# Sliding-window attention with a gated feed-forward on one core: GpSimd's clearings among VectorE's normalizations, dummy matmuls regrouped, reload waits added

## The chip, the core and the metric

The kernel runs on one core of one Trainium2 chip. Its time is the device time of one execution in microseconds; less is better. A run's time is that of a whole execution; a profile takes one execution apart, and its span is somewhat shorter than that execution's time.

## What is computed

`x` is 2048 x 576 (bf16). The result is `x + s * g`, both from the same normalized rows:

```python
xn = _layernorm(x, axis=-1)             # no scale, no shift
s = _A_ref(xn, A_wqkv, A_wo)            # attention, 32 heads of 18, window of 256 keys, causal, then wo
g = _silu(_B_ref(xn, B_w_gate, B_w_up, B_w_down))   # (sigmoid(xn Wg) * (xn Wu)) Wd, inner size 4608
return x + s * g
```

## The kernel before, in words

The 2048 rows are worked in four chunks of 512, each chunk in four blocks of 128 rows. A chunk goes through: layer norm and a transpose of the normalized rows (`xnr` to `xn`, so that the features lie on the partitions); projections to queries, keys and values; the feed-forward's gate and up projections with the attention's scores and products laid between their matmuls; the output projection and the down projection; the final combination. Weights stream from memory through rings of buffers on SyncE's DMA queue.

**Who sets the order.** The program is a list of operations (`Op`), each with an engine, a planned duration, dependencies `deps` (a semaphore wait where engines differ) and `odeps` (order for the planner alone: the operation is planned after them, but no wait is put into the program). `schedule` plays the list through with the planned durations and priorities (`prio`, lower goes first) and so fixes the order of the instructions on each engine; `emit` writes them out in that order and adds the waits. A wait that an engine has made before is not written again. `slack` is added to the planned landing of a DMA.

**The opening** is what the change touches, that is chunk 0 up to the first feed-forward matmul:

- For each of the four blocks, VectorE makes two statistics (`bn_stats`, L509 and L511, one for each half of a row) and their combination (L513); GpSimd takes a power of the variance for 1/sqrt (L516, `rstd`); VectorE normalizes (L526, a `tensor_scalar` from bf16 to bf16 with two scalars per row). TensorE transposes (L552, ten small matmuls), ScalarE copies the result from PSUM to `xn` (L565).
- Between these, TensorE runs dummy matmuls on a buffer of ones (`warm`, L422), in groups `w0`, `w1`, `w2` of 8, 3 and 2 pairs (`WARM`), and the first projections (L608), each in three steps such as `q0.0`, `q0.1`, `q0.2` for the queries of block 0. Step `.0` needs the first half of that weight matrix, step `.1` the rest, and so a wait for DMAs. The order on TensorE is written out by hand in the string `OPEN`; `t0` to `t3` are the transposes.
- Buffers have to be cleared or filled once: `pk` on ScalarE (L413, one activation that writes zeros); three parts of `expr`, as `ez0` on VectorE and `ez1`, `ez2` on GpSimd (L386, 128 x 1024 f32 each); the ones beside the values, `vones` and `vpad` on GpSimd (L408, L409); the mask `m64`, by a memset (L397) and three `affine_select` (L400) on GpSimd and a copy on VectorE (L403). Before, GpSimd's order is: identity matrix and small constants, `ez1`, the four powers, then `ez2`, the mask's memset, `vones`, `vpad`, the three selects. The list `op_late` puts `ez2`, the mask's memset and `vones` behind the last power.
- Projected queries and keys go from PSUM to `pk` and `expr` in halves on ScalarE and VectorE (L679), values to `vau` (L726). VectorE also copies some blocks of `xn` from one half of the partitions to the other (L576), for the feed-forward.

**Reloads.** The projection weights lie in one layout for chunk 0 and are loaded again in another for the later chunks (`build_again`, eight DMAs during chunk 0's feed-forward). In the later chunks each projection depends on all eight (L594). The projections of chunk 1 stand on TensorE between the two halves of chunk 0's down projection (L1152): its row blocks 0 and 1 come before them, blocks 2 and 3 after.

Of the kernel before, what the change touches and what calls it, by code (L numbers as in the profile page):

```python
# [9 lines left out]
H = 32  # L10
DH = 18
# [93 lines left out]
OC_SLACK = 3000.0  # L105
LATE_SLACK = 5000.0
LN_STEP = 8
OPEN = """w0 t0 w1 t1 q0.0 w2 q0.1 q1.0 q1.1 t2 q0.2 q1.2 q2.0 q2.1 v0.0 v0.1 t3 q2.2 v0.2 q3.0 q3.1 v1.0 v1.1 q3.2 v1.2
v2.0 v2.1 v3.0 v3.1 v2.2 v3.2 k0.0 k0.1 k1.0 k1.1 k0.2 k1.2 k2.0 k2.1 k3.0 k3.1 k2.2 k3.2"""
OPEN_Y = ("q2", "v0", "v2", "v3", "k2", "k3")  # L110
QKV_AGAIN = 15
AGAIN_PRIO = 6
N_FACTOR = 1.2
# [5 lines left out]
TH_PRIO = 0  # L119
HM_PRIO = -1  # L120
QKT_BEHIND = {3: 0, 4: 1}
WARM = (8, 3, 2)
X0_SLACK = (-250.0, 150.0, 400.0, 900.0)
QKV_SLACK = 300.0
X_PRIO = (-20, -19, -18, -7.9)
X_EXTRA = (1.0, 1.0, 1.3, 1.3)
Q_SLACK = 0.0
QKV_LOAD = (-8, -6, -7)
W_PRIO = (-5, -4, -3, -2)
WARM_NS = 427.0  # L130
# [101 lines left out]
class Builder:  # L232
# [16 lines left out]
    def op(self, eng, occ, fn, name, deps=(), prio=3, **kw):  # L249
        o = Op(eng, occ, fn, name, deps, prio, **kw)  # L250
        o.cidx = len(self.ops)
        self.ops.append(o)
        return o
# [78 lines left out]
    def build(self):  # L332
        self.r_xr = Ring(NXR)
        self.r_xnr = Ring(NXNR)
        self.r_xn = Ring(1)
        self.r_w = Ring(RW)
        self.r_t = Ring(RT)
        self.r_pk = Ring(RPK)
        self.r_exp = Ring(NEXP)
        self.r_s = Ring(RS)  # L340
        self.r_xf = Ring(RXF)
        self.r_kd = Ring(RKD)
        self.r_rec = Ring(RREC)
        self.r_bn = Ring(RBN)
        self.op_f1 = {}
        self.op_proj, self.op_open = [], {}
        self.build_init()
        self.op_pv = [[None] * NHG for _ in range(NCH)]
        self.op_sc = [[[] for _ in range(NHG)] for _ in range(NCH)]
        self.op_on = [[None] * NHG for _ in range(NCH)]  # L350
        self.op_mul = [[None] * NHG for _ in range(NCH)]
        self.all_kd = {}
        self.op_oc = [[[], []] for _ in range(NCH)]
        self.op_v = [None] * NQB
        self.op_tail = [None] * NHG
        self.op_hT = {}
        self.f2_last = None
        self.op_out = []
        for c in range(NCH):
            self.build_ln(c)  # L360
            if c == 0:
                self.build_weights()
                self.build_wd()
            self.build_qkv(c)
            self.last_mul = None
            self.build_attn(c)
            self.load_x(c)
            self.op_pkz = [self.op("POOL", 2000, lambda e: e.memset(self.pk[:, 1:RPK, :, :], 0.0), f"pkz:{c}",
                                   deps=self.op_on[c], prio=1)]
            if c == 0:  # L370
                self.op_wo = []
            self.build_wo(c)
            self.build_ffn(c)
            if c == 0:
                self.build_again()
                self.build_late_weights()
                for o in self.ops:
                    if o.name in ("wo:0:00", "wo:0:10"):
                        o.add_dep(self.op_wo)
                for k, o in enumerate(self.op_wo):  # L380
                    self.f2_ops[(1, k % 5)].add_dep(o)

    def build_init(self):
        op = self.op
        self.op_pre = op("DVE", 450, lambda e: e.memset(self.hT[:, 0, :], 1.0), "pre", prio=-9)
        ez = [op(eng, 1000, lambda e, k=k: e.memset(self.expf[:, 2 * k:2 * k + 2, :, :], 0.0), f"ez{k}", prio=p)  # L386
              for k, (eng, p) in enumerate((("DVE", -8), ("POOL", 0), ("POOL", 0)))]
        self.op_ez = ez
        self.op_negh = op("POOL", 60, lambda e: e.memset(self.neghalf[:, :], -0.5), "neghalf", prio=-5)
        ep = op("POOL", 60, lambda e: e.memset(self.bnst[:, :, 12:14], 0.0), "eps0", prio=-5)  # L390
        self.op_eps = op("POOL", 60, lambda e: e.memset(self.bnst[:, :, 14:15], EPS * D), "eps1", deps=[ep], prio=-5)
        id1 = op("POOL", 200, lambda e: e.memset(self.op_[:, NOT - 1, 0:P], 1.0), "id1", prio=-6)
        self.op_ident = op("POOL", 300, lambda e: e.affine_select(
            self.op_[:, NOT - 1, 0:P], self.op_[:, NOT - 1, 0:P], pattern=[[1, P]], compare_op=ALU.is_equal, fill=0.0,
            base=0, channel_multiplier=-1), "id2", deps=[id1], prio=-4)
        ez[1].odeps.append(self.op_ident)
        m1 = op("POOL", 300, lambda e: e.memset(self.m64[:, :, :], 1.0), "m1", prio=0)  # L397
        self.op_late = [ez[2], m1]
        for k in range(3):
            m1 = op("POOL", 200, lambda e, k=k: e.affine_select(  # L400
                self.m64[0:64, k, :], self.m64[0:64, k, :], pattern=[[-1 if k == 1 else 1, 64]], compare_op=ALU.is_ge,
                fill=0.0, base=-(k % 2), channel_multiplier=1 if k == 1 else -1), f"m2:{k}", deps=[m1], prio=3)
        self.op_mask = [op("DVE", 130, lambda e: e.tensor_copy(self.m64[64:P, :, :], self.m64[0:64, :, :]), "m3", deps=[m1],  # L403
                           prio=2)]
        h0 = op("DVE", 70, lambda e: e.memset(self.hm[:, :], 0.0), "hm", prio=4)
        self.op_hm = [op("DVE", 70, lambda e, q=q: e.memset(self.hm[32 * q:32 * q + 32, q % 2:q % 2 + 1], 1.0),
                         f"hm:{q}", deps=[h0], prio=4) for q in range(4)]
        vo1 = op("POOL", 1100, lambda e: e.memset(self.vau[:, :, :, 0:H // 2, DH:DH + 1], 1.0), "vones", prio=1)  # L408
        self.op_vones = op("POOL", 300, lambda e: e.memset(self.vau[:, :, :, H // 2, :], 1.0), "vpad", deps=[vo1], prio=1)  # L409
        self.op_late += [vo1, h0]  # L410
        for k, n in enumerate(WARM):
            self.op_open[f"w{k}"] = self.warm(n, f"warm:{k}", [self.op_pre] if k == 0 else [], mm_ns(CH) if k else WARM_NS)
        self.op_pkz = [op("ACT", 1300 + 1000, lambda e: e.memzero(self.pk[:, 0:2, :, :]), "pkz", prio=-30)]  # L413

    def warm(self, n, name, deps, ns):
        ps = Psum((6, 7))
# [21 lines left out]
    def build_weights(self):  # L438
        wq = self.wqkv
        self.op_wqn = [[] for _ in range(3)]  # L440
        for j in range(3):
            c0 = j * D
            nat = self.wqn[:, j, 0:4 * D].rearrange("p (k c) -> p k c", k=4)
            for k in (0, 2):
                r0 = k * P + (64 if k else 0)
                self.op_wqn[j].append(self.dma(
                    nat[:, k:k + 2, :], wq[r0:r0 + 2 * P, c0:c0 + D].rearrange("(k p) c -> p k c", p=P),
                    N_FACTOR * 2 * P * D * 2, f"wqn{j}.{k}", ("wqkv", j, k // 2), prio=QKV_LOAD[j], issue=W_ISSUE_NS))
            for h in range(2):
                self.op_wqn[j].append(self.dma(  # L450
                    self.wqn[64 * h:64 * h + 64, j, 4 * D:4 * D + HV], wq[MID * 64:MID * 64 + 64, c0 + h * HV:c0 + (h + 1) * HV],
                    W_FACTOR * D // 2 * P, f"wqn{j}.{4 + h}", ("wqkv", j, 2 + h), prio=QKV_LOAD[j]))
            for o in self.op_wqn[j]:
                o.slack = QKV_SLACK
        o = self.op_wqn[0][0]
        o.eng, o.prio, o.slack = "ACT", -40, Q_SLACK
        o.add_dep(self.op_pre)
        self.op_pkz[0].behind.append(o)
# [34 lines left out]
    def build_ln(self, c):  # L493
        op = self.op
# [3 lines left out]
        for i in range(QPC):  # L498
            st = c * QPC + i
            if c == 0:  # L500
# [6 lines left out]
                           prio=X_PRIO[i] if c == 0 else 4, slack=X0_SLACK[i] if c == 0 else LATE_SLACK)  # L507
# [16 lines left out]
            if c == 0:  # L524
                out = out.rearrange("p (g c) -> p g c", g=2)
            ap = op("DVE", 400 if c == 0 else 350, lambda e, st=st, xs=xs, out=out: e.tensor_scalar(  # L526
                out, xs, self.mv[:, st, 0:1], self.rstd[:, st, :], ALU.subtract, ALU.mult), f"apply:{st}",
                deps=[rs, ag] + dr, prio=pr)
            ring.release(sx, ap)
            if c > 0:  # L530
                wr = op("DVE", 100, lambda e, sr=sr: e.tensor_copy(self.xnr[:, sr, D:DP], self.xnr[:, sr, 0:64]),
                        f"wrap:{st}", deps=[ap], prio=pr)
            if st == QPC - 1:
                self.op_mask[0].odeps.append(ap)
                for o in self.op_late:
                    o.odeps.append(rs)
            tok = slice(i * P, (i + 1) * P)
            if c > 0:
                for k, (i0, i1, col) in enumerate(((0, NKT, 0), (NKT, NC, 64))):
                    o = self.dma(self.xn[:, i0:i1, tok], self.xnr[:, sr, col:col + (i1 - i0) * P],  # L540
                                 XT_BYTES * (i1 - i0) * P * P * 2, f"xt:{st}.{k}", ("xt", i, k), deps=[wr, ap] + dxn,
                                 prio=-2, issue=XT_ISSUE_NS, transpose=True)
# [975 lines left out]
```

## Time and profile before

| | |
|---|---|
| median of 3 runs | 560.14 us (560.14 to 560.2) |
| the profiled execution's own time | 560.04 us |
| its span | 558.3 us |
| TensorE busy (matmul) | 552.4 us, 99% |
| VectorE, ScalarE, GpSimd busy | 318.9, 274.9, 32.1 us |
| DMA | 74.24 MB, mean 133 GB/s |

The span runs from the first instruction to the last. An engine's busy time counts its compute instructions, not its waits. In a timeline each line gives start and duration in us, engine, source line, operation, output and inputs, count, and in brackets how long the engine stood idle before it and what ended that. PE is TensorE, PEld its weight loads, DVE VectorE, ACT ScalarE, POOL GpSimd, SP SyncE; a q behind a name is its instruction queue.

### The profile page before, as it was taken

How to read it: one execution, taken by the hardware profiler on the slowest of the kernel's cores; microseconds unless marked ns; L12 is line 12 of the kernel's file. 1: busy time of each engine (PE TensorE's matmuls, PEld its weight loads, DVE VectorE, ACT ScalarE, POOL GpSimd, SP SyncE). 2: the span in 40 equal slices, each digit the busy share in tenths (PEclk: the TensorE clock that was granted, in tenths of full speed). 3: DMA queues.
4: the chain of work that ended last, by engine and by line, in shares of the span. 5: the costliest groups of instructions: out<-in, count | busy, mean ns of one | idle time of the engine just before them, and what ended most of it. 6: DMA issues, size and time to landing. Idle time of an engine off the chain costs nothing.

```text
span 558.3 us, 18736 instructions
## 1 busy us (share of the span) xinstructions
PE 552.4 (99%) x8128; PEld 312.9 (56%) x8130; DVE 318.9 (57%) x906; ACT 274.9 (49%) x388; POOL 32.1 (6%) x61
## 2 busy tenths in 40 slices
PE   7999999999999999999999999999999999999998
PEld 4755555569555555546755555545665555554554
DVE  7536997506066986633507699844430785786111
ACT  4426786114066785702407678740330875774031
POOL 5001110100000110010000011001000000000100
PEclk9999999999999999999999999999999999999999
DMA  8999999936956765314995656422479365651010
GB/s 232 221 201 199 223 209 220 240 61 115 197 123 139 156 149 125 80 43 65 136 218 120 156 128 153 108 66 63 75 124 231 94 130 130 145 126 32 21 44 22
DMA packets 126058, 74.24 MB, mean 133 GB/s; under 512 B 54808, under 2 KB 125464, under 8 KB 125976
## 3 DMA queue, kind: packets, MB, share of 16 engines
q1 hardware_dynamic: 125704, 72.75, 62.0%
q8 instruction: 64, 1.05, 0.8%
q10 hardware_dynamic: 272, 0.29, 0.2%
q14 instruction: 18, 0.15, 0.1%
HBM read 56.37 MB, written 2.36 MB: 105 GB/s over the span
## 4 chain that ended last, share of the span: by engine, by line
PE 98%; DVE 1%; DMA 0%; issue 0%; ACT 0%; DVEq 0%
PE ps L1004 50%; PE ps L1152 22%; PE ps L588 7%; PE ps L790 6%; PE ps L847 4%; PE ps L917 3%; PE ps L608 2%; PE ps L1207 2%; PE ps L1183 2%; DVE xnr L526 0%; DMA xr<-in_A_x_dram 0%; PE ps L422 0%; PE ps L552 0%; DVE bnst L509 0%; DVE bnst L511 0%
## 5 line engine op out<-in xcount | busy, mean ns | idle before, releaser
L1004 PE MATMUL ps<-xn,wgs 64*128 64x512 bf16 x2522 | 299.7, 376 | 0.1
L1004 PEld LDWEIGHTS ps<-xn,wgs 64*128 64x128 bf16 x2522 | 122.4, 94 | 112.8 <-issue 1.4
L805 ACT ACTIVATE expr<-ps 128x1024 bf16<-128x1024 f32 (+1 forms) x152 | 150.6, 1019 | 20.7 <-PE ps L790 20.3
L1022 DVE SCALAR_TENSOR_TENSOR hT<-tring,ps 128x512 bf16<-128x512 bf16 x144 | 98.2, 682 | 55.2 <-PE ps L1004 35.4
L1018 ACT ACTIVATE tring<-ps 128x512 bf16<-128x512 f32 x144 | 86.5, 601 | 86.0 <-PE ps L1004 71.7
L1152 PE MATMUL ps<-wd_sb,hT 64*128 64x512 bf16 (+1 forms) x2016 | 125.5, 283 | 0.0
L1152 PEld LDWEIGHTS ps<-wd_sb,hT 64*128 64x128 bf16 x2016 | 65.8, 94 | 58.5
L819 DVE TENSOR_TENSOR expr<-expr,m 128x256 bf16<-128x256 bf16 (+1 forms) x272 | 60.8, 265 | 9.0 <-ACT expr L805 8.1
L790 PE MATMUL ps<-qkp,kd 64*128 64x320 bf16 (+3 forms) x720 | 56.9, 252 | 0.0
L790 PEld LDWEIGHTS ps<-qkp,kd 64*128 64x128 bf16 x720 | 34.4, 94 | 33.6 <-DVE pk L863 0.8
L773 DVE TENSOR_SCALAR kd<-qkp,hm 128x256 bf16<-128x256 bf16 x176 | 40.4, 290 | 14.8 <-DMA qkp<-pk 13.2
L1241 ACT ACTIVATE expr<-ps 128x576 bf16<-128x576 f32 (+2 forms) x17 | 9.8, 620 | 74.0 <-PE ps L1152 58.7
L1243 DVE SCALAR_TENSOR_TENSOR expr<-expr,ps 128x576 bf16<-128x576 bf16 x12 | 8.5, 750 | 66.0 <-ACT expr L1241 66.0
L942 ACT ACTIVATE sat<-ps 128x576 bf16<-128x576 f32 x16 | 9.5, 648 | 67.8 <-PE ps L917 67.8
L588 PE MATMUL ps<-wqkv_sb,xn 64*128 64x288 bf16 x648 | 40.7, 283 | 0.1
L588 PEld LDWEIGHTS ps<-wqkv_sb,xn 64*128 64x128 bf16 x648 | 33.0, 94 | 6.5 <-issue 0.2
L1245 DVE TENSOR_TENSOR expr<-expr,sat 128x576 bf16<-128x576 bf16 (+2 forms) x17 | 7.2, 436 | 43.5 <-ACT expr L1241 34.4
L863 DVE STREAM_TRANSPOSE pk<-ps 128x512 f32<-128x512 f32 x32 | 21.3, 693 | 16.3 <-PE ps L847 16.1
L829 POOL COPY qkp<-qkp 128x256 bf16<-128x256 bf16 x24 | 10.9, 456 | 255.5 <-DVE kd L773 255.5
L847 PEld LDWEIGHTS ps<-expr,vau 64*32 64x32 bf16 x1440 | 18.1, 92 | 7.8 <-issue 5.9
L880 DVE STREAM_TRANSPOSE op__63<-pk 128x512 bf16<-128x512 bf16 x32 | 22.3, 701 | 0.1
L847 PE MATMUL ps<-expr,vau 64*32 64x320 bf16 (+4 forms) x1440 | 20.8, 254 | 0.0
(59 smaller groups left out, 252.3 us busy)
## 6 DMA issues: line engine op xcount, KB each, us to landing
wgs<-in_B_w_gate_dram SPq DMA_DIRECT2D x47, 240.0 KB, 3.8
wgs<-in_B_w_up_dram SPq DMA_DIRECT2D x47, 240.0 KB, 5.0
wgs<-in_B_w_up_dram SPq DMA_DIRECT2D x47, 192.0 KB, 4.1
wgs<-in_B_w_gate_dram SPq DMA_DIRECT2D x47, 192.0 KB, 4.3
wd_sb<-in_B_w_down_dram SPq DMA_DIRECT2D x9, 576.0 KB, 5.9
xf<-in_A_x_dram SPq DMA_DIRECT2D x18, 144.0 KB, 4.2
out_dram<-xf SPq DMA_DIRECT2D x15, 144.0 KB, 4.6
xr<-in_A_x_dram SPq DMA_DIRECT2D x14, 144.0 KB, 4.6
```

Source lines behind the costliest of these rows:

```text
L588: r = e.matmul(self.bank(ps, HV, hf), self.xn[r0:r0 + 64, k, i * P:(i + 1) * P], self.wqn[r0:r0 + 64, j, c0:c0 + HV], start=(k == 0), stop ...
L773: return e.tensor_scalar(dst, src, self.hm[:, half:half + 1], None, ALU.mult)
L790: i = e.matmul(self.bank(ps, 512, r)[:, pos * 64:(pos + n) * 64], w, self.qkp[r0:r0 + 64, hg, q0 * 64:(q0 + n) * 64], start=True, stop=Tru ...
L805: return e.activation(self.expr[:, es, :, 0:ncol], src, ACTF.Exp, scale=SM_SCALE)
L819: return e.tensor_tensor(ap, ap, m, ALU.mult)
L847: r = e.matmul(self.bank(ps2[s_])[32 * cg:32 * cg + 32, q0 * 64:(q0 + n) * 64], vf[:, v0:v0 + 32], self.expr[p0:p0 + 64, es, cg % 2, pos * ...
L863: tr = self.rd("DVE", dve_ns(CH), lambda e, tf=tf, s_=s_: e.transpose(tf, self.bank(ps2[s_])), f"t1:{c}:{t}", deps=[o, self.op_mul[c][t - ...
L880: t2 = self.op("DVE", dve_ns(CH), lambda e, on=on: e.transpose(self.op_[:, hg % NOT, :], on.rearrange("p g d -> p (g d)")), f"t2:{c}:{hg}" ...
L1004: return e.matmul(self.bank((pg, pu)[gu][ft]), w, self.xn[r0:r0 + 64, k, :], start=first, stop=last, tile_position=(r0, 0))
L1018: return e.activation(self.tring[:, st_, :], self.bank(ps), ACTF.Tanh, scale=0.5)
L1022: return e.scalar_tensor_tensor(self.hT[:, ft, :], self.tring[:, st_, :], 1.0, self.bank(ps), ALU.add, ALU.mult)
L1152: r = e.matmul(self.ps[:, b + n0:b + n1], self.hT[r0:r0 + 64, ft, i * P:(i + 1) * P], self.wd_sb[r0:r0 + 64, q, ft % WDG, n0:n1], start=(s ...
```

## The change

Cut to its core:

```diff
-OPEN = """w0 t0 w1 t1 q0.0 w2 q0.1 ...
+OPEN = """w0 t0 w1 t1 w3 q0.0 w2 q0.1 ...
+VO_PRIO = -3
-WARM = (8, 3, 2)
-X0_SLACK = (-250.0, 150.0, 400.0, 900.0)
+WARM = (9, 1, 2, 1)
+X0_SLACK = (-250.0, 150.0, 400.0, 500.0)
+Q1_SLACK = 500.0
-Q_SLACK = 0.0
+Q_SLACK = 1900.0
...
                 for k, o in enumerate(self.op_wo):
                     self.f2_ops[(1, k % 5)].add_dep(o)
+                for k, o in enumerate(self.op_wqkv[0]):
+                    self.f2_ops[(3, k % 5)].add_dep(o)
...
-        ez = [op(eng, 1000, lambda e, k=k: e.memset(self.expf[:, 2 * k:2 * k + 2, :, :], 0.0), f"ez{k}", prio=p)
-              for k, (eng, p) in enumerate((("DVE", -8), ("POOL", 0), ("POOL", 0)))]
+        ez = [op(eng, 1000, lambda e, k=k: (e.memzero(self.expf[:, 2 * k:2 * k + 2, :, :]) if k == 2 else e.memset(self.expf[:, 2 * k:2 * k + 2, :, :], 0.0)), f"ez{k}", prio=p)
+              for k, (eng, p) in enumerate((("DVE", -8), ("POOL", 0), ("ACT", -29)))]
...
-        m1 = op("POOL", 300, lambda e: e.memset(self.m64[:, :, :], 1.0), "m1", prio=0)
-        self.op_late = [ez[2], m1]
+        m1 = op("POOL", 300, lambda e: e.memset(self.m64[:, :, :], 1.0), "m1", prio=-19)
+        self.op_late = []
+        self.op_m1 = m1
...
-                fill=0.0, base=-(k % 2), channel_multiplier=1 if k == 1 else -1), f"m2:{k}", deps=[m1], prio=3)
+                fill=0.0, base=-(k % 2), channel_multiplier=1 if k == 1 else -1), f"m2:{k}", deps=[m1], prio=-19)
+        self.op_m2 = m1
...
-        vo1 = op("POOL", 1100, ..., "vones", prio=1)
-        self.op_vones = op("POOL", 300, ..., "vpad", deps=[vo1], prio=1)
-        self.op_late += [vo1, h0]
+        vo1 = op("POOL", 1100, ..., "vones", prio=VO_PRIO)
+        self.op_vones = op("POOL", 300, ..., "vpad", deps=[vo1], prio=VO_PRIO)
+        self.op_late += [h0]
...
+        ez[2].odeps.append(self.op_pkz[0])
...
-                o.slack = QKV_SLACK
+                o.slack = Q1_SLACK if j == 0 else QKV_SLACK
...
+            if st == 1:
+                self.op_m1.odeps.append(ap)
+            if st == 2:
+                self.op_m2.odeps.append(ap)
```

What it makes of each engine's order in the built program:

- **GpSimd**: identity and constants, `vones`, `vpad`, `ez1`, two powers, the mask's memset and two selects, the third power, the last select, the fourth power.
- **ScalarE**: `ez2` as one more activation, right after the one that clears `pk`; the rest as before.
- **TensorE**: the dummies stand as 18, 2, 2 and 4 single matmuls (ahead of `t0`, between `t0` and `t1`, after `t1`, after `q0.0`) instead of 16, 6 and 4. One projection has one wait for ScalarE less. Everything else, and every other wait, is as before.
- **VectorE**: the same up to the eviction after the fourth normalization; then the mask's copy and the first two copies of `xn` come earlier, and the first values' block is evicted ahead of the third block of queries.
- **SyncE**: the same order and the same waits.

## The prediction

> **What bounds the kernel now.** I read the chain that ended last first: TensorE has 98% of it, so a microsecond saved counts only where TensorE stood still or did work that nobody uses. Then the waits of TensorE, all of them over the whole span (columns: in total, how often, the longest):
>
> ```profile
> PE ps L552 <- DVE xnr L526: 1.6, 2, 1.1
> PE ps L422 <- DVE hT L385: 1.5, 1, 1.5
> PE ps L1183 <- issue: 0.2, 1, 0.2
> ```
>
> The 1.5 is the start itself. The 1.6 are two waits of the opening's transposes (L552) for normalized rows (L526): 0.44 before the first, 1.12 before the fourth. Third, the timeline of the first 20 us (start, duration, engine, line, in brackets the idle time before):
>
> ```profile
> 5.18 0.63 POOL L516 TENSOR_TENSOR rstd<-mv,neghalf 128x1 f32<-128x1 f32 x1 [0.36 <-DVE mv L513]
> ...
> 5.55 0.45 PE L552 MATMUL ps<-op__63,xnr 64*128 64x64 bf16 x10 [0.44 <-DVE xnr L526]
> ...
> 5.79 1.41 PE L422 MATMUL ps<-hT 64*128 64x512 bf16 x6
> 5.92 0.45 DVE L526 TENSOR_SCALAR xnr<-xr,mv,rstd 128x640 bf16<-128x640 bf16 x1 [0.52 <-POOL rstd L516]
> ...
> 7.41 0.61 PE L422 MATMUL ps<-hT 64*128 64x512 bf16 x4
> ...
> 7.77 0.92 PEld L608 LDWEIGHTS ps<-wqkv_sb,xn 64*128 64x128 bf16 x16 [0.25 <-issue]
> ...
> 8.12 0.45 DVE L526 TENSOR_SCALAR xnr<-xf,mv,rstd 128x640 bf16<-128x640 bf16 x1 [0.76 <-PE ps L422]
> ...
> 8.97 2.38 PE L608 MATMUL ps<-wqkv_sb,xn 64*128 64x288 bf16 x36
> ...
> 10.13 0.95 POOL L386 MEMSET expr<- 128x1024 f32 x1
> ...
> 10.29 2.04 DVE L526 TENSOR_SCALAR xnr<-xf,mv,rstd 128x640 bf16<-128x640 bf16 x1
> ...
> 11.21 0.94 POOL L408 MEMSET vau<- 128x192 bf16 x1
> 12.21 0.35 POOL L409 MEMSET vau<- 128x228 bf16 x1
> ...
> 12.48 0.32 PE L552 MATMUL ps<-op__63,xnr 64*128 64x64 bf16 x10 [1.12 <-DVE xnr L526]
> ```
>
> The reader is to see the fourth normalization (10.29): the same work as at 5.92 and 8.12, 2.04 us instead of 0.45. It began after a GpSimd clearing (10.13), stood through three of them, and ended at 12.33, 0.18 after the one that ended at 12.15; the next clearing had to wait for that one, so GpSimd paused there. A later place shows the same, on VectorE and GpSimd:
>
> ```profile
> 382.18 1.80 POOL L368 MEMSET pk<- 128x2048 bf16 x1 [22.50 <-DVE op__63 L880]
> 382.55 1.60 DVE L526 TENSOR_SCALAR xnr<-xr,mv,rstd 128x576 bf16<-128x576 bf16 x1 [0.42 <-DMA xn<-xnr]
> ```
>
> It ended 0.17 after the clearing; its like takes 0.43. So a normalization that finds a clearing running ends about 0.18 after GpSimd's next pause. The Trainium skill (SBUF — State Buffer, "Who interferes with whom") says that VectorE in a two-port mode and GpSimd hold a shared port pair exclusively, and who comes first keeps it; both rows agree.
>
> **The parts, in order of time.** Positions are those of the built program of the changed kernel, durations those of the rows.
>
> *Clearings ahead (GpSimd).* The ones, the pad and the second score clearing now run from 1.39: 0.94 + 0.06 pause + 0.35 + 0.95, to about 3.65. GpSimd's first power (4.26) has 0.6 to spare. New neighbours are the first statistics (L509, 3.02). The trace has no statistics beside a clearing. Lower bound 0, as a statistics beside a GpSimd copy took 0.45 (82.89) like one alone; upper bound blocking to 3.65, which ends the first at 3.83 instead of 3.49, 0.34 on every later step of VectorE. A faster one has no reason. I take 0, the nearest row.
>
> *Third score clearing to ScalarE.* Like the one at L413, 1.06 us: 4.30 to 5.36. ScalarE was idle until 6.04; cover 0.68, cost 0.
>
> *Mask between the normalizations (GpSimd).* The edit orders these in the planner and adds no semaphore wait, so on the chip the mask's clearing starts when the second power ends: 5.76 to 6.02 (0.26), then two selects of about 0.4, each after a pause of 0.07, to 6.96; the third select comes after the third power, 7.93 to 8.34. The second normalization (5.92) therefore meets the clearing. If it gets in at the pause after 6.02 it could end at 6.20; its own 0.45 ends at 6.37 anyway: 0. Were it held through both selects, it would end at 6.96 + 0.18 = 7.14, 0.77 late. I take 0: VectorE's copies beside these selects (12.72, two in 0.88) took the 0.42 that they take alone, and the fourth normalization got in at the first pause. The third one, against a select that ends at 8.34, ends at 8.52 at the latest, before its own 8.57. Beside the fourth nothing is left: 10.29 + 0.45 = 10.74.
>
> *Dummies.* TensorE has 26 dummy matmuls in both kernels: 16, 6 and 4 become 18, 2, 2 and 4 (the 2 after the second transposes). A pair takes 0.427 at the start (weight loads at 1.92, 2.35, 2.78) and 0.216 later (L1004, 126 in 13.60); the second transposes, at 7.02, already run at the full pace (0.15 for ten instead of 0.24), and the pace doubles at about 6.98, where the sixth dummy's end puts it. The ninth first pair runs 4.91 to 5.34, inside the wait: 0. Then: first transposes 5.55 to 5.79, one pair to 6.20, wait for the second normalization (6.37 + 0.15 reaction, as 12.33 to 12.48) to 6.52, transposes to 6.75, one pair to 7.08, four projection matmuls 0.25 to 7.33, four dummies 0.43 to 7.76. Next are 16 matmuls that need the queries' weights: the last of these lands at 7.67 in the trace, and the load above, idle for 0.25, comes at 7.77. So they start at 7.80 instead of 7.845: of the removed dummies 0.05 is kept, that transfer eats the rest.
>
> *Third and fourth transposes.* 16 matmuls take 0.98: 8.78, where the third normalization allows 8.12 + 0.45 + 0.15 = 8.72. Ten transposes and 36 matmuls take 2.35 (8.825 to 11.175 before), so TensorE reaches the fourth at 11.13; the normalization allows 10.74 + 0.15 = 10.89. Before: 12.48. **Saved: 1.35 us**, and 0.24 of cover is left.
>
> *What is late next.* The fourth eviction (0.70 on ScalarE) keeps its distance to the transposes, and so does the stall of 0.1 behind it. VectorE evicts the values' first block ahead of the third query block, which then is free at about 13.8; its bank is wanted at 14.7 or later. VectorE's masks and copies move within idle time. SyncE's queue keeps its order; up to 21.8 us it issues without waiting for TensorE, and the feed-forward weights that are needed at 22.5 (then 21.15) landed at 16.98. The shortest lead of a later transfer over TensorE in the opening chunk is the last down weights: landed 107.48, used 109.49. Even if no transfer came earlier, 2.01 - 1.35 = 0.66 would remain.
>
> *Reload waits.* The new dependency goes to the second half of chunk 0's last down-projection pair. The built program has not one wait more or less there: the next chunk's projections stand ahead of it on TensorE and still wait for all eight reloads. This part does nothing; 0.
>
> **Sum.** All else is equal instruction for instruction. The profiled execution took 560.04 (span 558.3 and 1.74 around it): 560.04 - 1.35 = 558.69. The median of the three runs is 0.10 above it; so 558.79, or **558.8**.
>
> **Rivals.**
>
> 1. *GpSimd still holds VectorE.* Statistics blocked (0.34): third normalization at 8.46, transposes at 9.06, fourth at 11.41, saved 1.07: 559.1. Second normalization held through both selects (0.77): third at 8.89, transposes at 9.49, fourth at 11.84, saved 0.64: 559.5. Both: 0.3 saved, 559.8. For it: no row has statistics beside a clearing. Against: the rows above.
>
> 2. *TensorE's pace doubles later: slower.* Before, it stood 0.64 us (4.91 to 5.55) ahead of the doubling; now 0.21 and 0.32, and more of the rest are short transposes. If the wait at 6.20 starts the count anew, and it needs the 5.46 from first dummy (1.52) to doubling again, the pace doubles at 11.98: 6.75, 7.18, 7.67, 8.53 for the steps above, 16 matmuls at half pace 1.96 to 10.49, transposes to 10.73, five pairs by 11.98, the other 13 at 0.1225: fourth at 13.57, 1.1 later than before: 561.2. It breaks even for a doubling near 9.8. Against it: the three runs agree within 0.06, and TensorE stands still for less in sum. The Trainium skill (TensorE: Matmul & The Clock Gate, "What's actually happening" and Part 4) has a free-running activity window of about 3.4 us in which transposes do not count as busy. By that rule a missed window would put the doubling at 10.4 and the fourth transposes at 12.8, 0.3 late, an estimate of 560.4; no trace here shows a missed one.
>
> 3. *The gain is given back.* Weights fill the DMA queues through chunk 0 (share near 1 up to 100 us). If one transfer there shifts by 1.5 us against TensorE, the 0.66 is overdrawn by some 0.8: 559.6. Against it: every other lead is longer.
>
> That the change does not do what it says holds for the reload waits, at no cost either way.
>
> **How the numbers follow.** Forecast 0.68 (558.5 to 559.0), GpSimd 0.16 (559.0 to 559.8), given back 0.05, later doubling 0.08 (560.4 to 561.4), more than forecast 0.03, if a doubling comes earlier. The range takes in the single blockings and what is more: 558.4 to 559.6; outside lie the late doubling and a little of the rest. 0.2%, 1.12 us, is about what a measurement can tell from no change; 1.35 is just beyond it. Faster by that: forecast, more, and hardly any of the others, 0.70; slower: the far end of rival 2, 0.04; same: 0.26.
>
> **What would show it.** Right: no fourth wait of 1.1 at L552's fourth group, L526 at 0.4 to 0.5 four times, first 16 projection loads still at 7.77, a new wait of 0.3 before the second transposes, feed-forward at about 21.15. Rival 1: L509 or L526 over 0.5 before 7 us. Rival 2: projection pairs 0.24 apart after 7.1. Rival 3: a new wait of TensorE for a DMA. Wrong altogether: a start of feed-forward at 21.15 and an end that is not 1.35 earlier.

## The result, and the profile after

| | before | after |
|---|---|---|
| median | 560.14 us (560.09 to 561.55, 9 runs) | 558.46 us (558.15 to 559.93, 9 runs) |
| the profiled execution, its span | 560.04 us, 558.3 us | 558.46 us, 556.7 us |
| share of TensorE in the chain that ended last | 98% | 99% |
| GpSimd, VectorE, ScalarE busy | 32.1, 318.9, 274.9 us | 31.0, 316.9, 275.8 us |

The ratio is 0.9971, with a 95% interval of 0.996 to 0.9982: faster by 0.3%, or 1.68 us between the medians. The forecast was 558.8, from 558.4 to 559.6.

The waits of TensorE in the kernel after (in total, how often, the longest) have one row left, the start itself. The row for the transposes, with its two waits, is gone. (So is the row of 0.2 at L1183; it stands only in profiles that recorded 8128 of the 8130 matmuls, and that of the kernel before is one of these.)

```profile
PE ps L429 <- DVE hT L389: 1.5, 1, 1.5
```

The timeline of its opening (start, duration, engine, line):

```profile
1.40 0.94 POOL L414 MEMSET vau<- 128x192 bf16 x1
...
2.39 0.30 POOL L415 MEMSET vau<- 128x228 bf16 x1
2.62 0.96 POOL L390 MEMSET expr<- 128x1024 f32 x1
...
3.08 0.46 DVE L516 BATCH_NORM_STATS2 bnst<-xr 128x6 f32<-128x288 bf16 x1 [0.54 <-DMA xr<-in_A_x_dram]
...
4.22 1.04 ACT L390 ACTIVATE expr<-expr 128x1024 uint32<-128x1024 uint32 x1
...
5.82 0.25 POOL L401 MEMSET m<- 128x192 bf16 x1
...
5.98 0.45 DVE L533 TENSOR_SCALAR xnr<-xr,mv,rstd 128x640 bf16<-128x640 bf16 x1 [0.52 <-POOL rstd L523]
...
6.48 0.45 PE L563 MATMUL ps<-op__63,xnr 64*128 64x64 bf16 x10
...
7.54 0.59 PE L429 MATMUL ps<-hT 64*128 64x512 bf16 x4
...
7.75 1.04 PEld L619 LDWEIGHTS ps<-wqkv_sb,xn 64*128 64x128 bf16 x16
...
7.97 1.14 PE L619 MATMUL ps<-wqkv_sb,xn 64*128 64x288 bf16 x16
...
8.18 0.45 DVE L533 TENSOR_SCALAR xnr<-xf,mv,rstd 128x640 bf16<-128x640 bf16 x1 [0.77 <-PE ps L429]
...
10.35 0.45 DVE L533 TENSOR_SCALAR xnr<-xf,mv,rstd 128x640 bf16<-128x640 bf16 x1
...
11.30 0.31 PE L563 MATMUL ps<-op__63,xnr 64*128 64x64 bf16 x10
```

What to see: the fourth normalization (10.35) takes 0.45, like the second and third. GpSimd has nothing long beside it; its clearings lie at 1.40 to 3.58, and the first statistics (3.08), which run beside the last of them, take the 0.46 that they take alone. The mask's clearing (5.82) meets the second normalization and costs it nothing.

Stage by stage, in the two profiled executions, TensorE is ahead by 1.18 us at the fourth transposes (11.30 against 12.48) and by 1.19 at the first feed-forward matmul (21.32 against 22.50). So far it is the change at work. But at the first attention scores (near 47 us) it is ahead by 1.47, and after 459 us by 1.58, and no instruction between was changed. The rest of this text is mostly about this growth of some 0.4 us.

Two pauses that TensorE makes in the kernel before and not in the kernel after make up 0.36 of it. Two feed-forward matmuls there start 0.488 us apart (35.90 and 36.39) where 0.216 is the rule, and a feed-forward matmul and the score matmul behind it 0.309 (459.24 and 459.55). In the first place a multiplication of VectorE is late; it empties the bank that TensorE wants, and TensorE goes on 0.14 after its end (36.25). The timelines of both kernels there, before:

```profile
33.19 0.69 DVE L1022 SCALAR_TENSOR_TENSOR hT<-tring,ps 128x512 bf16<-128x512 bf16 x1 [1.25 <-ACT tring L1018]
...
35.56 0.69 DVE L1022 SCALAR_TENSOR_TENSOR hT<-tring,ps 128x512 bf16<-128x512 bf16 x1 [1.68 <-PE ps L1004]
```

and after:

```profile
33.95 0.69 DVE L1033 SCALAR_TENSOR_TENSOR hT<-tring,ps 128x512 bf16<-128x512 bf16 x1 [1.25 <-ACT tring L1029]
...
35.89 0.69 DVE L1033 SCALAR_TENSOR_TENSOR hT<-tring,ps 128x512 bf16<-128x512 bf16 x1 [1.25 <-ACT tring L1029]
```

The idle time ahead of the multiplication is 1.68 instead of 1.25. The bracket names TensorE as what ended it, but by the count of the semaphore TensorE's matmuls for it were done at 34.35, and ScalarE's factor at 35.03 (34.43 + 0.60): half a microsecond in which VectorE waited for nothing that the profile shows. The second pause begins the same way: a multiplication at 456.19 starts after 0.33 of idle time, VectorE then works without a gap, and the scaled keys that the score matmul needs are done at 459.41, where TensorE already stands.

### The profile page after: what moved, and what is told of

Its sections match the earlier page's. It is cut to its first block, busy times and chain, and to the rows that moved or that the text cites. A ratio compares the mean times of both kernels' runs of the same rounds, so it can differ in the third digit from the quotient of the medians.

```text
span 556.7 us, 18736 instructions
## 1 busy us (share of the span) xinstructions
PE 552.6 (99%) x8130; PEld 313.1 (56%) x8130; DVE 316.9 (57%) x906; ACT 275.8 (50%) x389; POOL 31.0 (6%) x60
## 3 DMA queue, kind: packets, MB, share of 16 engines
q8 instruction: 64, 1.05, 0.9%
## 4 chain that ended last, share of the span: by engine, by line
PE 99%; DVE 0%; issue 0%; ACT 0%
PE ps L1015 50%; PE ps L1163 22%; PE ps L599 7%; PE ps L801 6%; PE ps L858 4%; PE ps L928 3%; PE ps L619 2%; PE ps L1194 2%; PE ps L1218 2%; PE ps L429 1%; PE ps L563 0%; DVE hT L389 0%; ACT expr L1252 0%; DVE expr L1256 0%; DVE xf L1258 0%
## 5 line engine op out<-in xcount | busy, mean ns | idle before, releaser
L1163 PEld LDWEIGHTS ps<-wd_sb,hT 64*128 64x128 bf16 x2016 | 67.0, 94 | 57.3
```

What stands on the lines that cost most here:

```text
L1163: r = e.matmul(self.ps[:, b + n0:b + n1], self.hT[r0:r0 + 64, ft, i * P:(i + 1) * P], self.wd_sb[r0:r0 + 64, q, ft % WDG, n0:n1], start=(s ...
```

## The experiments

The kernels ran in three groups, each on one chip beside the kernel before (medians 560.16, 560.12 and 560.13). Line numbers below are each kernel's own.

**Both kernels again.** First question: do the pauses at 36 and 459 us belong to the program, or to the one execution that was profiled? The kernel before, unchanged:

> The kernel before, once more with a profile of its own. Its first profile has a normalization of 2.04 us at 10.29 and a lone late VectorE multiplication at 35.56, after which TensorE stood still 0.27 us longer than its cadence. Theory (the fourth normalization alone carries the change's gain; the late multiplication belongs to one execution): the 2.04 us comes again, fourth transposes at 12.48, time 560.1 to 560.2; the pause of 0.27 us near 36 us need not come again. Rival (the pause near 36 us belongs to the kernel, and the change removes it too): it comes again at the same place.

Measured: 560.07 (559.92 to 560.87, 11 runs), ratio 0.9999 [0.9991, 1.0008]. The profiled execution has both pauses again, 0.489 us (36.27 to 36.76) and 0.310 (459.67 to 459.98), and the same late multiplication. They belong to the program. The kernel after, unchanged:

> The changed kernel once more. Its nine times stand in three groups, 558.15 to 558.20, 558.46 to 558.52 and 559.81 to 559.93; its profiled execution took 558.46, and in it the matmul pace doubles at 7.43 us (before: 6.98). Theory (the groups are different moments of the doubling): a profile whose time is near 558.17 has the doubling near 7.0 and the fourth transposes near 11.1, one near 559.85 has it near 10.4 to 10.8 and the transposes near 12.8. Rival (the groups come from memory or from later stages): the moments in the first 12 us are the same whatever the time, and the difference lies later.

Measured: 558.32 (558.12 to 560.77, 12 runs), ratio 0.9973 [0.9964, 0.9982]. Neither pause is there. This time the profile caught one of its longer executions, 559.60. Its opening is as forecast (fourth transposes 11.13, feed-forward 21.15), with the doubling of the clock at 4.97, not at the 10.4 to 10.8 that the theory needs; the microsecond was lost later. The timeline of TensorE has two stops for which nothing is named:

```profile
76.57 0.82 PE L1015 MATMUL ps<-xn,wgs 64*128 64x512 bf16 x6 [0.39 <-issue]
...
83.98 0.26 PE L858 MATMUL ps<-expr,vau 64*32 64x128 bf16 x10 [0.53 <-issue]
```

Start to start they are 0.765 instead of 0.216 and 0.750 instead of 0.056, together 1.24 us: that execution was long for these, not for a late clock. The first of them is seen once more, smaller (0.396, in the third profile of the kernel after, which ran below); in the other profiled executions there is neither. What they are stays open; the last section says where they lie.

**The parts.** The clearings alone: the kernel after with the old dummies.

```diff
-OPEN = """w0 t0 w1 t1 w3 q0.0 w2 q0.1 ...
-WARM = (9, 1, 2, 1)
+OPEN = """w0 t0 w1 t1 q0.0 w2 q0.1 ...
+WARM = (8, 3, 2)
```

> The changed kernel with the dummy matmuls of before (16, 6 and 4, none after the second transposes); clearings and everything else as changed. Theory (clearings carry the gain): fourth normalization 0.45 us, second transposes at 7.0 to 7.05, third at 8.8 to 8.9, fourth at 11.15 to 11.25, time 558.2 to 558.9. Rival (the regrouped dummies carry a good part): fourth transposes no earlier than 11.6, time 558.9 or more.

Measured: 558.25 (558.19 to 558.91, 5 runs), ratio 0.9967 [0.9954, 0.998]. The fourth transposes of its profiled execution (558.60, with the doubling at 7.45) start at 11.45, later than expected. The dummies alone: the kernel before with the new `WARM` and `OPEN`.

> The kernel before with only the dummy matmuls regrouped (18, 2, 2 and 4). Theory: the fourth normalization still starts behind the clearing at 10.13 and ends at 12.33, so the fourth transposes stay at 12.48 and the time at 560.1 to 560.2 (0.0 gained). Rival (the regrouped dummies carry a good part): 559.8 or less.

Measured: 560.16 (559.97 to 560.41, 11 runs), ratio 1.0 [0.9991, 1.0008]. The fourth normalization in its timeline is as long as ever, and the fourth transposes start at 12.75, 6.92 after the first ones, as in the kernel before (the second block of rows landed at 4.28 here, at 3.46 there, and all behind it lies 0.27 later):

```profile
10.56 2.04 DVE L526 TENSOR_SCALAR xnr<-xf,mv,rstd 128x640 bf16<-128x640 bf16 x1 [0.29 <-POOL rstd L516]
```

So the clearings carry the whole gain, the later 0.36 included (their program has no pause at 36 or 459 us either, that of the dummies has both), and the dummies nothing. Without the reload waits the built program is the same, instruction for instruction.

**The place in VectorE's stream.** The programs seen so far with the pauses have one instruction more on VectorE than those without: 1140 against 1139 as built. It is the wait for GpSimd's ones and pad ahead of the first block of values, needless now that these stand ahead of powers which VectorE has waited for. (The section on the change counts every other wait as before; this one it missed.) Counted in the trace, the late multiplication at 35.56 us is VectorE's 64th instruction, and those that are late near 456 and 501 us are the 960th and the 1088th: 64 plus a multiple of 128. In the kernel after, the 64th is the semaphore instruction ahead of that multiplication, where VectorE waits anyway. To try this, one instruction was added to each kernel, with some 60 ns of work near 17 us, and no other change:

```diff
-        h0 = op("DVE", 70, lambda e: e.memset(self.hm[:, :], 0.0), "hm", prio=4)
+        h0 = op("DVE", 70, lambda e: [e.memset(self.hm[:, k:k + 1], 0.0) for k in range(2)][-1], "hm", prio=4)
```

The kernel after with it:

> The kernel after, with the zeroing of the 128x2 mask of heads (line 411) done as two instructions of 128x1 in place of one: VectorE's stream gets one instruction more, some 60 ns of work near 16.5 us, off the path, and every later instruction of VectorE stands one place further back, as in the kernel before. All engines' order is otherwise the same. Theory of the place in the stream: VectorE's 64th, 960th and 1088th instruction of the trace are then again the multiplications that started 0.43, 0.4 and 0.41 us late in the kernel before, so TensorE's pauses of 0.27 us (near 34.3 us) and 0.09 us (near 457.7 us) come back, and the time is that of after plus 0.36, 558.3 + 0.36 = 558.66 (558.5 to 558.9). Rival, that the pauses went because the clearings moved (other times of the engines, other traffic): no pause, 558.3 (558.2 to 558.45).

Measured: 558.65 (558.54 to 560.21, 10 runs), ratio 0.9978 [0.9968, 0.9987], 0.2 to 0.4 above the medians of the kernel after. Both pauses are back, 0.497 us (34.50 to 35.00) and 0.310 (457.85 to 458.16), with the same instruction late:

```profile
34.16 0.69 DVE L1033 SCALAR_TENSOR_TENSOR hT<-tring,ps 128x512 bf16<-128x512 bf16 x1 [1.69 <-PE ps L1015]
```

The kernel before with it:

> The kernel before, with the zeroing of the mask of heads (line 405) done as two instructions in place of one: one instruction more for VectorE, some 60 ns of work, nothing else changed. Theory of the place in the stream: the multiplications that started late step one place on, the place of the delay falls on the waiting instruction ahead of them, where VectorE idles anyway, and both of TensorE's pauses (0.27 near 36.3 us, 0.09 near 459.5 us) go: 560.16 - 0.36 = 559.80 (559.65 to 560.0), although the kernel does more. Rival: the pauses belong to the old place of the clearings, and stay: 560.16 to 560.2.

Measured: 559.78 (559.63 to 560.68, 11 runs), against 560.12 for the kernel before beside it. The ratio, 0.9997 [0.9988, 1.0006], does not separate them by itself; but 8 of the 11 times lie below the lowest of the 26 of the kernel before (559.96), and the trace has neither pause:

```profile
35.88 0.69 DVE L1022 SCALAR_TENSOR_TENSOR hT<-tring,ps 128x512 bf16<-128x512 bf16 x1 [1.25 <-ACT tring L1018]
```

The same is seen in TensorE's busy time in one stretch (length, then PE busy). The kernel before, the kernel after, the kernel after with one instruction more, and the kernel before with one more:

```profile
33.00:37.50 4.50, 4.39 (x44) 1.00 1.25 159
```

```profile
33.00:37.50 4.50, 4.50 (x44) 1.00 1.17 200
```

```profile
33.00:37.50 4.50, 4.38 (x42) 1.00 1.38 151
```

```profile
33.00:37.50 4.50, 4.50 (x45) 1.00 1.15 219
```

One instruction more brings the pauses into one kernel and takes them out of the other. That is the place, and not the clearings' time: the theory holds and its rival falls.

**The price of the clock.** The second rival of the prediction had TensorE's clock double later if TensorE does less ahead of it. In the kernel after, the last four pairs of the first group of dummies were cut to 32 columns, so that TensorE stands idle for 1.65 us ahead of the first transposes:

```diff
-                    r = e.matmul(self.bank(ps, CH, hf), self.hT[r0:r0 + 64, 0, 0:P], self.hT[r0:r0 + 64, 0, :],
+                    c = 32 if name == "warm:0" and k >= 5 else CH
+                    r = e.matmul(self.bank(ps, c, hf), self.hT[r0:r0 + 64, 0, 0:P], self.hT[r0:r0 + 64, 0, 0:c],
```

> The kernel after, with the last four pairs of the first nine pairs of dummies at 32 columns in place of 512 (numbers kept): TensorE is busy for about 2.1 us less, from some 3.7 to 5.1 us it stands idle. Theory of the prediction's second rival: the doubling of the granted clock needs TensorE busy ahead of it, and comes one measuring stretch later, near 10 to 11 us; the projections up to there run at half the rate, the fourth pair of transposes starts at 12.6 to 12.8 in place of 11.1 to 11.3: 559.4 to 560.0. Theory of a free moment: the doubling came at 4.97 to 10.10 us in the executions seen with the same dummies, so the amount of dummies does not set it, and 558.3 to 558.6 comes out.

Measured: 559.93 (559.02 to 560.61, 11 runs), ratio 0.9994 [0.9986, 1.0003]: all but 0.2 us of the gain is gone. The profile caught the shortest execution, with the doubling at 8.58 us (10 to 11 was expected), the 16 projection matmuls 0.50 later than in the kernel after and the fourth transposes 0.56 later:

```profile
8.47 1.20 PE L620 MATMUL ps<-wqkv_sb,xn 64*128 64x288 bf16 x16
...
11.86 0.31 PE L564 MATMUL ps<-op__63,xnr 64*128 64x64 bf16 x10
```

The amount of dummies does matter; the theory of a moment that does not depend on it falls. That a still later doubling makes the median is argued: no such execution was profiled. But the moment is not fixed by the dummies either. By the trace's records of the clock, and by the pace of the matmuls where there is none, it came between 4.53 and 7.45 us in eleven of the thirteen profiled executions whose first group is full (eight or nine pairs), and at 10.10 and 10.89 us in two, both with the kernel before's opening (560.48 and 560.50, where the medians were 560.07 and 559.78). TensorE's matmuls in one stretch show it, the kernel before in its first profile and the same opening with one instruction more on VectorE:

```profile
8.00:10.00 2.00, 2.00 (x46) 1.00 0.98 305
```

```profile
8.00:10.00 2.00, 2.00 (x18) 1.00 0.99 319
```

18 matmuls in place of 46 in 2 us, with TensorE busy throughout; the next column, the granted clock, says 1.00 in both. (Ten of the 46 are short transposes, so the counts overstate it: pairs of projection matmuls start 0.24 us apart before the doubling at 10.89 and 0.12 after it.) The Trainium skill (TensorE: Matmul & The Clock Gate, "What's actually happening") has a free-running activity window of about 3.4 us; a spread of 2.9 us, and two that came 2.7 and 3.4 us after its end, agree with that.

**A longer clearing beside a normalization.** In the kernel after, GpSimd clears one more block (0.95 us) straight ahead of the mask's small one:

```diff
-        m1 = op("POOL", 300, lambda e: e.memset(self.m64[:, :, :], 1.0), "m1", prio=-19)
+        def f_m1(e):
+            e.memset(self.expf[:, 6:8, :, :], 0.0)
+            return e.memset(self.m64[:, :, :], 1.0)
+        m1 = op("POOL", 300, f_m1, "m1", prio=-19)
```

> The kernel after, with one more clearing for GpSimd, 128x1024 elements of 4 bytes (such a one took 0.96 us in after, line 390), straight ahead of the mask's small clearing that follows the first normalization (line 401, 5.82 to 6.07); so GpSimd clears from some 5.85 to 7.05 us, in place of 0.25 us, while VectorE's second normalization (5.98 to 6.42) is due. Theory, a normalization is held as long as GpSimd clears: it ends about 0.15 after GpSimd's clearings, near 7.1 to 7.25 (it takes 1.1 to 1.25 us in place of 0.446); the second pair of transposes, the third and the fourth normalization follow 0.5 to 0.8 later, and the time is 558.8 to 559.1. Rival, only the old clearings of 2 us did harm, or the hold has to do with the place of the buffer: the normalization takes 0.45 and the time is 558.2 to 558.45.

Measured: 558.78 (558.67 to 562.73, 11 runs), 0.53 above the kernel after beside it (558.25). Its timeline:

```profile
5.84 0.95 POOL L402 MEMSET expr<- 128x1024 f32 x1
5.99 0.97 DVE L536 TENSOR_SCALAR xnr<-xr,mv,rstd 128x640 bf16<-128x640 bf16 x1 [0.52 <-POOL rstd L526]
6.73 0.43 POOL L403 MEMSET m<- 128x192 bf16 x1
```

The normalization takes 0.97 and ends 0.18 after the first clearing; the small one behind it took 0.43 instead of 0.25. So it is held, as the theory says, but by one clearing, not by both, and it ended at 6.96 where 7.1 to 7.25 was expected. In the kernel before three clearings that followed each other as closely held one for 2.04. What decides between these is open. Four of the times are 560.24 to 560.43; none of those was profiled.

**The last dummies.** In the kernel after's profile the 16 projection matmuls start at 7.97, behind four dummies that began at 7.54. One pair of them was cut to 32 columns:

```diff
+                    c = 32 if name == "warm:2" and k == 1 else CH
```

> The kernel after, with the second pair of dummies behind the first projection matmuls at 32 columns in place of 512 (their number is kept, so every later instruction keeps its place). In after the 16 first projection matmuls start at 7.97 us in the profiled execution, behind these dummies, not at the 7.80 that the weights' landing (7.67) allows. Theory A, the end of the first projections is set by that dummy pair: they start at 7.75 to 7.82, and the second pair of transposes and all behind it moves ahead by 0.05 to 0.18 as far as the third normalization allows (its end 8.63 + 0.15 = 8.78 against 8.95): 558.1 (558.0 to 558.25). Theory B, the pace of TensorE is set by the moment of the clock's doubling, which comes at another time in each execution: the pair matters only in executions in which it runs at the half clock, and the median stays 558.3 (558.2 to 558.4).

Measured: 558.14 (558.09 to 558.42, 5 runs), ratio 0.9964 [0.9952, 0.9977]; the 16 matmuls start at 7.35, earlier than theory A had it, and the third transposes (8.58) then wait for the third normalization (its end 8.52), as in theory A. It ran again beside the kernel after, and with the pair ahead of the projections cut too:

> The kernel after with the one short pair of dummies, once more, beside the kernel after on the same chip. Theory: 558.14 again, 0.1 to 0.3 below the kernel after. Rival: the five executions seen were by chance those without a late clock or a pause, and it is level with the kernel after (558.3, some executions at 559 and over).

> The kernel after, unchanged: 558.3 (558.1 to 558.5), with one execution in four or five at 559 to 560.

> The kernel after, with both the second pair behind the first projection matmuls and the new pair ahead of them at 32 columns (numbers kept). With the first of the two alone the projections' 16 matmuls started at 7.35 us in place of 7.97 and the second transposes waited for the third normalization (8.53) to 8.58, so the path lies with VectorE there: theory, the second cut gives nothing more, 558.14 (558.0 to 558.3). Rival, less work for TensorE ahead of 7 us puts the doubling of its clock off, as it did with the four short pairs (559.93): 558.8 to 559.6.

Measured: 558.18 (558.14 to 558.23) with one pair short, 558.25 (558.13 to 558.59) for the kernel after, 558.17 (558.15 to 558.47) with two short, 5 runs each; ratios to the kernel before 0.9965 [0.9953, 0.9978], 0.9967 [0.9954, 0.9979] and 0.9965 [0.9952, 0.9979]. The short pair has the lowest medians of all, but the kernel after is within what can be told apart, and the second cut adds nothing. In the profile of the unchanged kernel the fourth transposes started at 11.06, in that of the short pair at 11.03.

## Why the prediction was right, and where it was not

- **The wait for the fourth normalization.** Right: 0.45 in place of 2.04, and no wait left. The clearings ahead cost nothing (statistics 0.46 and 0.44 beside one), the one moved to ScalarE nothing (4.22 to 5.26), the mask's nothing (second normalization 0.446). Rival 1 did not happen. Its price was real, though: a clearing of 0.95 us in the mask's place costs 0.53.
- **The dummies.** Forecast 0.05 kept; alone they gave nothing that can be measured. The step took the doubling at 6.98 in the kernel after too, because three runs agreed within 0.06. But the moment is not tied to a dummy's end: in the kernel after it came at 7.43, 4.97 and, in the third profile, between 5.86 and 6.50, and the fourth transposes at 11.30, 11.13 and 11.06, where 11.13 was forecast. The wait of 0.3 for the second normalization is there (0.34) only with the doubling at 4.97. Nor did the queries' weights set the start of the 16 matmuls, as the step had it: they landed at 7.22 in the kernel after, not at 7.67, and with one pair short (landing 7.21) the matmuls started at 7.35.
- **The opening's sum.** 1.35 was forecast; 1.18, 1.34 and 1.42 were measured at the fourth transposes against the kernel before's first profile (12.48). Counted from each profile's own first transposes, which leaves out when the rows landed, it is 1.23, 1.49 and 1.49: less than forecast with the doubling at 7.43, and more where TensorE, not held up by the weights, reached the third normalization's end.
- **"All else is equal instruction for instruction."** This step failed. It overlooked that VectorE has one wait fewer, and took equal work to mean equal time. That wait shifted VectorE's stream by one place, and the pauses at 36 and 459 us went: 0.27 + 0.09 = 0.36 more. With it the sum is 560.14 - 1.35 - 0.36 = 558.43 against a median of 558.46; with the measured 1.49 it is 558.29, and the other two medians of the kernel after are 558.32 and 558.25. That the range held the result is luck in part: its lower end, 558.4, was set for an earlier doubling, and not for this.
- **What is late next.** Right: nothing. No transfer ate the gain, the feed-forward began at 21.32, 21.15 and 21.08, where 21.15 was forecast, and rival 3 did not happen.
- **Rival 2.** Not in any profiled execution of the kernel after; with TensorE idle for 1.65 us ahead of it the doubling came at 8.58 in the shortest execution, and the median rose to 559.93. Some executions of the kernel after took 559 to 560; one of them was profiled, and was long for another reason. Whether a late clock makes the others is open.
- **The reload waits.** Right: the built program is the same without them.

## What to carry to other kernels

When a short instruction takes several times what its like takes, look at what GpSimd clears at that moment, and move the clearing to where the other engine waits for data anyway. Follow a forecast shift through all stages: where it grows between stages that were not touched, something else went, and a single added instruction can tell whether it is the instruction's place in its stream. A difference of a few tenths of a microsecond between two versions may be such a place, not the edit.

## What the runs showed of the hardware that was not expected

- **A late instruction at places 128 apart.** In four kernels VectorE's instructions at places 64, 448, 832, 960 and 1088 of its trace, all of them the feed-forward's multiplication, started 0.40 to 0.48 us after the semaphore instruction ahead of them, instead of 0.045 (the median of some 205 such pairs); the same multiplication at places 256, 384 and 640 started in 0.045. At the other places of 64 plus a multiple of 128 no such delay is seen: VectorE still worked on what came before, or waited there anyway. It costs time only where TensorE waits for that result: those at 448 and 832 (201.58 and 368.97 us, in the kernel before with one instruction more) held nothing up. That a fetch of instructions lies behind it is argued, not shown: the profile's page has 18 packets, 0.15 MB, on an instruction queue, some 8 KB each. The Trainium skill (Runtime: NRT & Kernel Launch, "Instruction fetch mechanics") has refills in blocks of 256 instructions, mostly hidden; the period here is 128, and two of the delays cost TensorE 0.36 us.
- **The doubling of TensorE's clock** came at 4.53 to 10.89 us with eight or nine full pairs of first dummies. The kernel before is hardly touched by it, because the wait for the fourth normalization hides it: with the doubling at 10.10 instead of 6.99, its fourth transposes started 0.37 later, and 0.30 of that was there at the first transposes already (5.85 against 5.55), where the second block of rows had landed at 4.30 instead of 3.46. That landing lengthens single executions with either opening: it came at 4.15 to 4.30 in five of the fourteen profiles and at 3.46 to 3.93 in the others; among the five is the one of 558.47 with two short pairs, whose median is 558.17.
- **Two stops of TensorE** of 0.55 and 0.69 us more than the usual step, near 76 and 84 us in one execution, the first also in another with 0.18, with nothing named. Counted in the trace, they lie behind TensorE's instructions 1985 and 2241, weight loads included: 256 places apart. The page has 64 packets, 1.05 MB, on another instruction queue, 16 KB each. That a late fetch of instructions makes these stops too is argued, not shown.
